# A new hand-written order of work in a fused attention and token-mixing kernel: first load ahead of the identity, q of the last batch loaded ahead of its k

## The chip, the cores and the metric

The kernel runs on one core of one Trainium2 chip. The metric is the time of one execution on the device in microseconds (us), as the median of three runs. Before the change it is 103.11 us (102.85 to 103.24).

The core has five engines with a queue each. TensorE (PE) multiplies matrices and writes to PSUM, an accumulator memory of eight banks. VectorE (DVE) and ScalarE (ACT) do the elementwise work and empty PSUM. GpSimd (POOL) does elementwise work in SBUF, the main on-chip memory. SyncE (SP) here only issues transfers. Each engine works through its queue in order and waits there until what the next instruction needs is done. Transfers (DMA) run beside the engines.

## What is computed

```
# per batch b (4) and head h (8); S = 768 rows, D = 64, 8 blocks of 96 rows
P = sort_net; five times: P = exp(P - rowmax); P /= rowsum; P /= columnsum   # 8x8, Sinkhorn
k_sorted = P @ k over blocks;   v_sorted = P @ v over blocks
attn = softmax(q_block @ k_sorted_block^T / 8)                               # inside a block
x[b, :, h] = attn @ v_sorted_block                                           # x: 768 x 512
# token mixing per batch
wq = x @ w_q;  wk = x @ w_k                                                  # 768 x 64
mixed = (wq @ wk^T / 8) @ x
out = relu(mixed) @ w_out                                                    # 768 x 512, float32
```

The inputs q, k and v are float32, 1.5 MB per batch each; the loads turn them into bf16.

## The kernel before

All work is cut into small **units**, and a table of words, `ORDER` (lines 17 to 46), says in which order they are recorded. A word such as `K30:0` has a kind (`K`), the batch (3), a number (0), and behind the colon what it works with. Capital kinds are matmuls on PE, and their number behind the colon is the PSUM bank. Small kinds empty the bank: `k30:A:0` empties bank 0 on ACT (`D` is DVE, `G` is POOL). `R`, `D` and `s` with `:S` are transfers that SP issues, and words with `l` are loads that POOL issues: `lq3` is q of batch 3, `lp` the two small mixing weights, `lo` the output weight. The order on each engine is the order of the table, restricted to that engine. Nothing reorders it later.

For one batch the units run as follows.

- `c`, `a` (batch-independent, at the start): the Sinkhorn iterations on a 32 x 64 tile `Pm`, on DVE (`c`, lines 167 to 181) and ACT (`a`, line 157), one waiting for the other. The last `c` leaves `PbT`. `B` and `n` spread it into the matrices `M` (lines 217 to 240), which every sorting matmul needs.
- `Q`/`q`: PE turns q of a pair of heads round, the result goes to `QT`. `K`/`k`: PE sorts k with `M`, into `KT`. `V`/`v`: the same for v, into `Vs`. Six `R` transfers (line 299) then bring `Vs` into blocks, `VT`. Batch 0 takes another way for v, by PE alone (`Y`, `y`, `F`, `f`).
- For batch 3, q is not turned by PE. POOL regroups it in four copies (`C`, line 358, into the buffer of another batch's q), and SP turns each copy round by a DMA transpose (`D34` to `D37`, line 362) into `QT`.
- `S`/`e`: scores and their exponential, seven units (E tile). `P`/`r`/`x`: attention times v, the reciprocal of the row sum, the normalised x; five units. `T`/`t`: x turned round, by PE, for batch 3 by DMA transposes (`D30` to `D33`).
- `J`/`j`/`d`, `W`/`w`, `G`/`g`, `H`/`h`, `O`/`o`: the token mixing, the last of them the output matmul, six units of four 128x512 matmuls. `s` stores to DRAM.

`Z` units are filler matmuls on a zero tile `fil`, whose results nobody reads. There are 28 of them, all in the first 14 us. `i00` makes the identity `idb` on POOL, `i02` clears tiles on DVE (`fil` among them), `i03` clears tiles on POOL.

There are three buffers for q, k and v each, so the loads of batch 3 go to the buffers of batch 0. All loads are issued by POOL, in the table's order: q0 v0 k0, v1, k1, q1, weights, q2 v2, output weight, k2, v3, k3, q3.

Of the kernel before, what the change touches and what calls it, by code (L numbers as in the profile page):

```python
# [16 lines left out]
ORDER = """
i00:G lq0 lv0 c00:D p01:A i02:D a01:A lk0 Z03:0 c01:D Z03:0 i03:G B01:0 a02:A Z014:1 c02:D lv1 a03:A c03:D
a04:A c04:D Q02:1 Q00:2 Q03:7 a05:A Z08:3 p00:A:0 q00:A:2 c05:D q02:A:1 q03:A:7 B00:0 Q01:3 n00:D:0 n02:D:0
n01:D:0 Y02:6 n03:D:0 Y00:1 y02:A:6 u00:D:0 Y01:4 y00:D:1 n10:G Y03:6 y01:D:4 F02:0 y03:A:6 F00:1 lk1 q01:A:3  # L20
f02:D:0 n11:G f00:D:1 K00:6 K01:2 k00:A:6 K03:0 k01:D:2 K02:4 lq1 k03:A:0 S00:6 k02:D:4 S02:2 e00:A:6 lp S01:0
F03:4 e01:A:0 S04:6 f03:D:4 lq2 F01:5 e02:A:2 P00:0 f01:D:5 n21:G e04:A:6 S03:2 r00:D:0 S06:4 x00:D:0 e03:A:2
P01:6 lv2 e06:A:4 r01:D:6 S05:0 x01:D:6 n20:G P02:2 e05:A:0 V10:4 r02:D:2 v10:A:4 x02:D:2 P03:0 lo K13:6 lk2
r03:D:0 P04:4 k13:A:6 x03:D:0 K12:2 lv3 V11:6 k12:A:2 r04:D:4 T01:0 x04:D:4 T00:1 v11:A:6 K11:2 t00:D:1 K10:4
k11:A:2 t01:D:0 V12:6 lk3 T03:1 k10:A:4 T02:0 lq3 t03:A:1 Q13:2 t02:D:0 Q12:3 Q11:4 v12:A:6 n31:G q12:D:3
J01:0 q13:D:2 J00:3 R15:S q11:D:4 j01:A:0 n30:G R11:S S13:6 j00:D:3 S14:0 R14:S e13:A:6 Q10:4 d00:G W00:3
R10:S W01:5 e14:A:0 w00:D:3 S15:6 R13:S w01:D:5 G00:3 d01:D q10:D:4 e15:A:6 R12:S S12:0 S10:4 G01:3 e12:A:0
Q22:7 g00:D:3 e10:A:4 q22:D:7 H01:0 H00:2 Q20:6 h01:A:0 h00:D:2 S11:4 e11:A:4 H02:0 S16:2 h02:D:0 Q23:7
e16:A:2 V22:4 q23:A:7 V20:2 v22:D:4 V21:0 O00:7 v20:A:2 q20:D:6 O02:4 o00:D:7 R20:S O03:2 o02:A:4 v21:A:0
P14:6 P11:3 r14:D:6 O01:5 x14:D:6 o03:A:2 R22:S r11:D:3 P13:6 R25:S x11:D:3 o01:A:5 P12:0 R23:S Q21:2 r13:D:6  # L30
R21:S r12:D:0 K23:3 x13:D:6 q21:A:2 O04:5 R24:S k23:A:3 x12:D:0 K21:6 K20:2 k21:A:6 o04:D:5 P10:0 k20:A:2
S22:6 r10:D:0 T13:5 x10:D:0 e22:A:6 T11:4 K22:2 t11:D:4 t13:A:5 S26:0 S21:6 k22:D:2 T12:4 e26:A:0 T10:5
e21:A:6 V31:0 t12:D:4 t10:D:5 S20:2 S23:6 e20:A:2 J11:5 J10:4 e23:A:6 j11:D:5 v31:D:0 S24:2 j10:A:4 W11:5
P21:6 e24:A:2 W10:4 r21:D:6 R33:S S25:0 w11:D:5 w10:A:4 x21:D:6 P20:2 e25:A:0 R32:S O05:4 r20:D:2 x20:D:2
V32:0 o05:A:4 P22:6 v32:A:0 P24:4 d10:D C30:G r22:D:6 T20:2 r24:D:4 G10:3 x24:D:4 t20:A:2 C31:G D34:S K30:0
x22:D:6 P23:4 k30:A:0 d11:G G11:3 r23:D:4 D35:S x23:D:4 K31:6 g10:A:3 K32:0 k31:A:6 C32:G H10:2 R35:S k32:D:0
V30:4 h10:A:2 R34:S T23:7 C33:G v30:D:4 T21:6 D36:S t23:A:7 T22:0 O10:2 t21:A:6 t22:D:0 R31:S H11:3 o10:D:2
S31:0 R30:S S32:6 e31:A:0 h11:D:3 J20:5 D37:S J21:2 e32:A:6 H12:0 s00:S j21:D:2 S33:3 j20:A:5 s02:S K33:6
e33:A:3 d21:D s01:S d20:G W20:5 k33:D:6 O11:2 h12:A:0 w20:D:5 W21:3 o11:D:2 S36:4 S34:6 e36:A:4 P31:0 s10:S
e34:A:6 G20:2 r31:D:0 w21:D:3 x31:D:0 S35:4 P32:6 e35:A:4 G21:2 r32:D:6 x32:D:6 S30:0 g20:A:2 P33:3 e30:A:0  # L40
O15:2 r33:D:3 D31:S x33:D:3 P34:0 o15:A:2 O12:7 r34:D:0 D32:S x34:D:0 P30:2 o12:A:7 H21:4 r30:D:2 H20:0 D33:S
x30:D:2 O13:7 h20:A:0 O14:6 h21:A:4 o13:D:7 D30:S O20:0 o14:D:6 O23:7 s12:S o20:A:0 s11:S O22:6 o23:D:7 J30:0
o22:D:6 J31:7 j30:A:0 s21:S O21:6 j31:A:7 d31:G W30:7 W31:0 o21:A:6 w30:D:7 H22:3 w31:D:0 G30:7 d30:D s20:S
h22:A:3 G31:7 O25:0 g30:D:7 H32:6 o25:D:0 H30:2 H31:4 h32:A:6 h30:D:2 O24:1 O34:7 o24:A:1 h31:D:4 O35:0 s22:S
o34:D:7 O30:4 o35:A:0 s34:S O33:7 s35:S o30:A:4 O32:0 s30:S o33:D:7 O31:4 s33:S o32:D:0 s32:S o31:D:4 s31:S
"""


# [605 lines left out]
```

## Time and profile before

| | us |
|---|---|
| median of three runs | 103.11 (102.85 to 103.24) |
| the profiled execution | 103.77 |
| its span in the profile | 101.9 |
| PE busy | 88.3 |
| DVE busy | 71.0 |
| ACT busy | 66.5 |
| POOL busy | 31.1 |

The profile follows one execution. The span runs from the first to the last record; 1.9 us of the execution lie outside it. An engine's busy time is the time in which at least one of its instructions ran; a matmul's end is modelled, so it can hold short waits. Times in the rows count from the start of the span. The lines that matter follow in the prediction.

### The profile page before, as it was taken

The page shows a single profiled execution, that of the slowest core. Times are in us where ns is not written, and L with a number is a line of the kernel's source. Part 1 is how long each engine was busy: PE and PEld are TensorE (multiplying, and loading weights), DVE is VectorE, ACT ScalarE, POOL GpSimd, SP SyncE. Part 2 cuts the span into 40 slices and gives each one's busy share as a digit, 9 for nine tenths or more (in the row PEclk, how much of TensorE's full clock was granted, in tenths as well). Part 3 has the DMA queues.
Part 4 walks back from the last instruction along what each step waited for, and adds up shares of the span by engine and source line. Part 5 has one row for each costly group of instructions (what it writes and reads, how often), then busy time and mean ns, then how long its engine had stood idle before and what let it go on. Part 6 is the DMA issues. An engine that isn't in the chain of part 4 may idle for free.

```text
span 101.9 us, 3335 instructions
## 1 busy us (share of the span) xinstructions
PE 88.3 (87%) x1403; PEld 60.0 (59%) x1412; DVE 71.0 (70%) x143; ACT 66.5 (65%) x92; POOL 31.1 (31%) x50
## 2 busy tenths in 40 slices
PE   0799989988998998799999999995799999999900
PEld 0234657887896676647687789753576544644300
DVE  0776559969976358928995899984769854477520
ACT  7212537999997699836799988975687653644200
POOL 7940007999969500000000006801000000860000
PEclk9999999999999999999999999999999999999998
DMA  0799999999999999999999991656998979824980
GB/s 3 71 193 203 203 206 206 184 192 204 198 194 202 203 225 245 247 204 222 218 242 240 205 220 31 130 134 143 264 413 302 119 160 361 357 113 175 346 308 6
DMA packets 25281, 20.63 MB, mean 202 GB/s; under 512 B 8240, under 2 KB 23344, under 8 KB 25264
## 3 DMA queue, kind: packets, MB, share of 16 engines
q0 software_dynamic: 14064, 10.09, 66.0%
q1 hardware_dynamic: 11200, 10.31, 33.4%
q8 instruction: 11, 0.18, 0.7%
q14 instruction: 6, 0.05, 0.1%
HBM read 20.19 MB, written 6.29 MB: 260 GB/s over the span
## 4 chain that ended last, share of the span: by engine, by line
DMA 46%; PE 33%; POOL 5%; DVE 4%; issue 3%; ACT 2%; SPq 1%; POOLq 0%; DVEq 0%
DMA Qn<-in_q_dram 41%; PE ps L142 33%; DMA QT<-Qn 4%; POOL M L238 3%; ACT mixT L417 2%; POOL Kn L214 2%; DMA Pm<-in_sort_net_dram 2%; DVE M L238 1%; DVE ot L148 1%; SPq L300 1%; POOL Qn L359 1%; POOL qD L380 1%; DVE PTR L148 0%; DVE KT L148 0%; DVE fil L190 0%
## 5 line engine op out<-in xcount | busy, mean ns | idle before, releaser
L314 ACT ACTIVATE E<-ps 96x960 bf16<-96x960 f32 (+1 forms) x28 | 23.6, 904 | 3.5 <-PE ps L142 3.5
L142 PE MATMUL ps<-wo,mixT 128*128 128x512 bf16 x88 | 22.0, 379 | 1.1 <-DMA wo<-in_moe_w_out_dram 0.6
L343 DVE TENSOR_TENSOR X<-ps,Rall 96x896 bf16<-96x896 f32 (+1 forms) x20 | 19.9, 1003 | 0.5
L142 PEld LDWEIGHTS <-mixT 128*128 128x128 bf16 x96 | 8.6, 97 | 10.4 <-DMA wo<-in_moe_w_out_dram 0.8
L148 DVE COPY ot<-ps 128x512 f32<-128x512 f32 x13 | 9.0, 690 | 5.3 <-PE ps L142 5.0
L146 ACT CAST KT<-ps 128x768 bf16<-128x768 f32 x13 | 10.2, 801 | 3.2 <-PE ps L142 2.9
L142 PE MATMUL ps<-fil 128*128 128x512 bf16 x27 | 9.1, 502 | 3.3 <-DVE fil L190 3.2
L142 PEld LDWEIGHTS <-KT 64*128 64x128 bf16 (+1 forms) x288 | 8.9, 97 | 5.0 <-issue 3.3
L359 POOL COPY Qn<-Qn 128x768 bf16<-128x768 bf16 x4 | 3.2, 826 | 26.8 <-DMA Qn<-in_q_dram 26.8
L142 PE MATMUL ps<-VT,E 96*128 96x65 bf16 x256 | 10.8, 193 | 0.4 <-ACT E L314 0.3
L142 PE MATMUL ps<-QT,KT 64*128 64x96 bf16 x256 | 9.4, 204 | 1.9 <-DMA QT<-Qn 1.1
L238 POOL TENSOR_TENSOR M<-PTR,m_p 128x512 bf16<-128x512 bf16 x6 | 7.9, 1330 | 9.7 <-DVE PTR L148 9.6
L142 PEld LDWEIGHTS <-E 96*128 96x128 bf16 x256 | 9.5, 97 | 2.3 <-issue 0.5
L146 ACT COPY ot<-ps 128x512 f32<-128x512 f32 x11 | 6.5, 588 | 6.5 <-PE ps L142 6.5
L380 POOL COPY qD<-qkT 64x384 bf16<-64x384 bf16 x4 | 2.0, 500 | 21.3 <-ACT qkT L146 20.4
L417 ACT ACTIVATE mixT<-ps 128x1024 bf16<-128x1024 f32 x7 | 7.0, 1021 | 2.2 <-PE ps L142 2.1
L142 PEld LDWEIGHTS <-fil 128*128 128x128 bf16 x28 | 3.1, 120 | 7.6 <-DVE fil L190 3.2
L148 DVE CAST KT<-ps 128x768 bf16<-128x768 f32 x7 | 6.5, 951 | 1.5 <-PE ps L142 1.5
L142 PE MATMUL ps<-M,Kn 128*64 128x128 bf16 x192 | 7.4, 221 | 0.0
L338 DVE RECIPROCAL Rall<-ps 96x14 f32<-96x14 f32 (+1 forms) x20 | 4.4, 226 | 3.2 <-PE ps L142 3.0
L142 PEld LDWEIGHTS <-Kn 128*64 128x64 bf16 x192 | 6.0, 109 | 1.0 <-issue 0.4
L146 ACT CAST Vs<-ps 128x1024 bf16<-128x1024 f32 x6 | 6.1, 1021 | 0.5 <-DMA VT<-Vs 0.4
(79 smaller groups left out, 136.2 us busy)
## 6 DMA issues: line engine op xcount, KB each, us to landing
out_dram<-ot SPq DMA_DIRECT2D x9, 512.0 KB, 3.3
Qn<-in_q_dram POOLq DMA_DIRECT2D x4, 768.0 KB, 11.2
Vn<-in_v_dram POOLq DMA_DIRECT2D x4, 768.0 KB, 15.3
Kn<-in_k_dram POOLq DMA_DIRECT2D x4, 768.0 KB, 16.9
VT<-Vs SPq DMA_DIRECT2D x18, 132.0 KB, 6.6
out_dram<-ot SPq DMA_DIRECT2D x6, 256.0 KB, 2.4
wo<-in_moe_w_out_dram POOLq DMA_DIRECT2D x1, 512.0 KB, 16.9
wqk<-in_moe_w_q_dram POOLq DMA_DIRECT2D x1, 64.0 KB, 9.5
```

The lines of the kernel that those rows point to most:

```text
L142: nc.tensor.matmul(o, w, x, is_transpose=t, start=start, stop=stop, skip_group_check=True)
L146: nc.scalar.copy(o, i)
L148: nc.vector.tensor_copy(o, i)
L214: nc.gpsimd.dma_start(out=t[b % NIN][:, h0:h1].rearrange("p h r d -> p h (r d)"), in_=src[b, h0:h1].rearrange("h (p r) d -> p h (r d)", p=P))
L238: ENG[e].tensor_tensor(out=M[b % 2][:, h0:h0 + hn], in0=src.unsqueeze(2).to_broadcast([P, hn, SP, NB]), in1=m_p.unsqueeze(1).unsqueeze(3). ...
L300: ENG[e].dma_start(out=VT[b % 2].rearrange("(s r) i h x -> r s i (h x)", r=R6)[n], in_=Vs[0][:, n].rearrange("p h e -> p (h e)"))
L314: nc.scalar.activation(E[b % 2][:, n, 0:2 * w * BLK].rearrange("p (t a c) -> p a t c", a=2, c=BLK), PS[0:BLK, bank:bank + 2, 0:w * BLK].re ...
L338: nc.vector.reciprocal(Rall[:, b, n, :, 0:w], avps(bank, w)[:, :, :, D])
L343: nc.vector.tensor_mul(xo.rearrange("p (a t d) -> p a t d", a=2, d=D), avps(bank, w)[:, :, :, 0:D], Rall[:, b, n, :, 0:w].unsqueeze(3).to_ ...
L359: nc.gpsimd.tensor_copy(pairs(b, n).rearrange("p (r h d) -> p r h d", r=R6, h=2), Qn[b % NIN][:, 2 * n:2 * n + 2].rearrange("p h r d -> p ...
L380: nc.gpsimd.tensor_copy(o, i)
L417: nc.scalar.activation(o, i, ACT.Relu)
```

## The change

The table is written anew: the order of the units, their banks and the engines that empty them. No function is touched, and the work is the same but for the fillers, of which there are 22 instead of 28. Of the evictions, ACT takes 17 of the 24 output evictions `o` (11 before) and DVE 7; ACT takes all four `y` (two before), five of eight `w` (one), two of eight `d` (none) and seven of nine `v` (six); DVE takes eight of sixteen `k` (five before), nine of twelve `t` (seven) and five of eight `j` (three). The word-for-word change of the table's first and last lines:

```diff
-i00:G lq0 lv0 c00:D p01:A i02:D a01:A lk0 Z03:0 c01:D Z03:0 i03:G B01:0 a02:A Z014:1 c02:D lv1 a03:A c03:D
+i02:D lq0 Z03:0 c00:D i00:G Z03:0 a01:A lv0 c01:D p01:A lk0 Z03:0 a02:A lv1 c02:D Z04:0 lk1 a03:A c03:D i03:G
...
-o34:D:7 O30:4 o35:A:0 s34:S O33:7 s35:S o30:A:4 O32:0 s30:S o33:D:7 O31:4 s33:S o32:D:0 s32:S o31:D:4 s31:S
+s22:S O34:7 o35:D:0 O30:4 s35:S o34:A:7 O33:0 s34:S o30:D:4 O32:7 s30:S o33:A:0 O31:4 s33:S o32:A:7 s32:S
+o31:A:4 s31:S
```

Three places show what moves. The first is POOL's queue at the start of the program. Before:

```order
L185 MEMSET idb_115 128x128
L186 ISA
L186 AFFINE_SELECT idb_115<-idb_115 128x128
L214 DMA Qn0_69<-in_q_dram 128x8x384
L214 DMA Vn0_75<-in_v_dram 128x8x384
L214 DMA Kn0_72<-in_k_dram 128x8x384
L195 MEMSET E0_87 96x7x32
```

And with the change (line numbers are one higher throughout):

```order
L215 DMA Qn0_69<-in_q_dram 128x8x384
L186 MEMSET idb_115 128x128
L187 ISA
L187 AFFINE_SELECT idb_115<-idb_115 128x128
L215 DMA Vn0_75<-in_v_dram 128x8x384
L215 DMA Kn0_72<-in_k_dram 128x8x384
L215 DMA Vn1_76<-in_v_dram 128x8x384
L215 DMA Kn1_73<-in_k_dram 128x8x384
L196 MEMSET E0_87 96x7x32
```

The load of q for batch 0 now stands ahead of the two instructions that make the identity, and the loads of v and k for batch 1 ahead of the clearing of tiles.

The second place is POOL's queue from the load of q for batch 2 (before) or from the load of k for batch 2 (after) up to the last load; buffers 0 to 2 of `Qn`, `Kn`, `Vn` hold batches 0 to 2, and batch 3 goes to buffer 0 again. Before:

```order
L214 DMA Qn2_71<-in_q_dram 128x8x384
L238 TENSOR_TENSOR M0_107<-PTR_110,m_p_116 128x512
L214 DMA Vn2_77<-in_v_dram 128x8x384
L238 TENSOR_TENSOR M0_107<-PTR_110,m_p_116 128x512
L209 DMA wo_79<-in_moe_w_out_dram 128x4x512
L214 DMA Kn2_74<-in_k_dram 128x8x384
L214 DMA Vn0_75<-in_v_dram 128x8x384
L214 DMA Kn0_72<-in_k_dram 128x8x384
L214 DMA Qn0_69<-in_q_dram 128x8x384
```

With the change:

```order
L239 TENSOR_TENSOR M0_107<-PTR_110,m_p_116 128x512 x2
L215 DMA Kn2_74<-in_k_dram 128x8x384
L210 DMA wo_79<-in_moe_w_out_dram 128x4x512
L215 DMA Vn2_77<-in_v_dram 128x8x384
L215 DMA Qn2_71<-in_q_dram 128x8x384
L215 DMA Vn0_75<-in_v_dram 128x8x384
L215 DMA Qn0_69<-in_q_dram 128x8x384
L215 DMA Kn0_72<-in_k_dram 128x8x384
```

Batch 2 is loaded as k, v, q instead of q, v, k, the output weight one place further forward; of batch 3, q now comes second and k last.

The third place is SP's queue from the last two `R` transfers that stand ahead of the first transpose of q for batch 3. Before:

```order
L300 DMA VT1_86<-Vs0_84 16x8x528 x2
L364 DMA_TRANSPOSE QT1_81<-Qn1_70 128x6x128 x2
L300 DMA VT1_86<-Vs0_84 16x8x528 x2
L364 DMA_TRANSPOSE QT1_81<-Qn1_70 128x6x128
L300 DMA VT1_86<-Vs0_84 16x8x528 x2
L364 DMA_TRANSPOSE QT1_81<-Qn1_70 128x6x128
L435 DMA out_0_dram<-ot0_103 128x1024
```

With the change:

```order
L301 DMA VT1_86<-Vs0_84 16x8x528 x2
L365 DMA_TRANSPOSE QT1_81<-Qn1_70 128x6x128
L301 DMA VT1_86<-Vs0_84 16x8x528
L365 DMA_TRANSPOSE QT1_81<-Qn1_70 128x6x128
L301 DMA VT1_86<-Vs0_84 16x8x528
L365 DMA_TRANSPOSE QT1_81<-Qn1_70 128x6x128
L301 DMA VT1_86<-Vs0_84 16x8x528 x2
L365 DMA_TRANSPOSE QT1_81<-Qn1_70 128x6x128
L436 DMA out_0_dram<-ot0_103 128x1024
```

The four transposes keep their place between the same transfers, roughly; what they wait for, the load of q for batch 3, is no longer the last load. On PE, the last load is waited for by `K30`. Behind `K30` the table now has 58 of PE's units, 61 before: `P23`, `T21`, `T22` and `V30` moved ahead of it, `T20` behind it.

More of the change, by code (lines that the diff above doesn't have):

```diff
@@ L17 @@
 ORDER = """
-i00:G lq0 lv0 c00:D p01:A i02:D a01:A lk0 Z03:0 c01:D Z03:0 i03:G B01:0 a02:A Z014:1 c02:D lv1 a03:A c03:D
[L19 to L42, printed above, removed]
@@ L43 @@
-o22:D:6 J31:7 j30:A:0 s21:S O21:6 j31:A:7 d31:G W30:7 W31:0 o21:A:6 w30:D:7 H22:3 w31:D:0 G30:7 d30:D s20:S
-h22:A:3 G31:7 O25:0 g30:D:7 H32:6 o25:D:0 H30:2 H31:4 h32:A:6 h30:D:2 O24:1 O34:7 o24:A:1 h31:D:4 O35:0 s22:S
-o34:D:7 O30:4 o35:A:0 s34:S O33:7 s35:S o30:A:4 O32:0 s30:S o33:D:7 O31:4 s33:S o32:D:0 s32:S o31:D:4 s31:S
+i02:D lq0 Z03:0 c00:D i00:G Z03:0 a01:A lv0 c01:D p01:A lk0 Z03:0 a02:A lv1 c02:D Z04:0 lk1 a03:A c03:D i03:G
+Z03:0 lq1 a04:A c04:D Q03:0 Q02:7 Q01:6 q03:D:0 a05:A Z06:5 c05:D Q00:5 B01:0 q00:D:5 B00:1 p00:A:0 q02:A:7
@@ new lines @@
+n01:D:1 n02:D:1 q01:A:6 Y01:4 n00:D:1 n03:D:1 y01:A:4 Y00:2 u00:D:1 Y03:6 Y02:4 n10:G y03:A:6 F01:0 y02:A:4
+F03:7 f01:D:0 lp y00:A:2 f03:D:7 K01:0 K00:2 k01:A:0 n11:G K03:6 k00:D:2 K02:4 k03:A:6 S02:0 k02:D:4 F02:2
+n21:G e02:A:0 S01:6 f02:D:2 S06:3 e01:A:6 S00:0 n20:G F00:5 e06:A:3 V12:6 f00:D:5 e00:A:0 S04:2 lk2 v12:D:6
+P01:4 e04:A:2 S05:0 lo r01:D:4 e05:A:0 R15:S P00:6 x01:D:4 lv2 S03:2 R14:S V10:0 e03:A:2 r00:D:6 lq2 P03:4
+x00:D:6 v10:A:0 P04:2 lv3 r03:D:4 r04:D:2 K12:6 x03:D:4 P02:0 k12:A:6 x04:D:2 V11:4 r02:D:0 T03:7 x02:D:0
@@ new lines @@
+v11:A:4 T00:6 K11:2 t00:D:6 T01:0 R12:S lq3 k11:A:2 t03:D:7 T02:4 R11:S t01:A:0 Q13:6 Q11:7 lk3 R10:S Q12:5
+t02:A:4 q11:D:7 Q10:0 R13:S K13:1 q10:A:0 J00:7 n31:G q12:A:5 S12:3 j00:D:7 J01:0 e12:A:3 k13:D:1 d00:G W00:7
+j01:A:0 q13:D:6 K10:3 w00:A:7 d01:D n30:G k10:A:3 S14:0 S13:6 W01:2 e13:A:6 w01:D:2 K21:3 G00:2 e14:A:0
+k21:D:3 S10:6 e10:A:6 K22:0 K20:3 k22:D:0 G01:2 k20:A:3 S11:6 g00:D:2 K23:0 e11:A:6 H01:2 k23:D:0 h01:A:2
+P12:4 S16:6 S15:0 r12:D:4 e16:A:6 x12:D:4 P10:2 e15:A:0 O03:7 r10:D:2 x10:D:2 o03:A:7 V22:0 H00:4 v22:A:0
@@ new lines @@
+V20:6 h00:D:4 P11:2 v20:A:6 R25:S V21:0 r11:D:2 H02:4 x11:D:2 v21:A:0 R20:S P13:6 R21:S h02:A:4 r13:D:6 P14:0
+x13:D:6 T11:2 R23:S Q20:3 R24:S Q21:4 r14:D:0 q20:A:3 Q23:7 R22:S q21:D:4 Q22:6 x14:D:0 S21:3 q22:A:6 O05:5
+q23:D:7 e21:A:3 t11:D:2 T13:7 S22:0 t13:D:7 S20:3 e22:A:0 T12:6 O04:7 t12:D:6 e20:A:3 T10:6 o04:A:7 S24:0
+t10:D:6 S26:2 O00:4 e26:A:2 o05:D:5 e24:A:0 V30:6 o00:A:4 S23:2 v30:D:6 S25:0 J10:5 e25:A:0 J11:4 R31:S
+j10:A:5 P21:0 e23:A:2 R30:S d10:G W10:7 V32:5 r21:D:0 j11:A:4 x21:D:0 P23:2 w10:A:7 O02:4 v32:A:5 C31:G
@@ new lines @@
+r23:D:2 x23:D:2 P22:0 d11:A C33:G o02:A:4 P20:6 W11:5 r22:D:0 V31:2 x22:D:0 C30:G w11:A:5 D37:S O01:4 v31:A:2
+C32:G r20:D:6 P24:0 x20:D:6 T22:5 o01:A:4 T21:2 R35:S t22:A:5 G10:3 r24:D:0 t21:D:2 D36:S K30:6 x24:D:0 K32:4
+k30:A:6 G11:3 k32:D:4 K33:0 R33:S g10:A:3 K31:6 k33:A:0 D35:S H10:2 k31:D:6 T20:4 h10:A:2 T23:5 S35:0 R34:S
+t23:D:5 S34:6 e35:A:0 H12:2 t20:D:4 R32:S O10:5 D34:S h12:A:2 J20:0 o10:D:5 e34:A:6 J21:1 j20:D:0 s00:S S36:4
+s02:S S32:2 j21:D:1 S33:6 e36:A:4 s01:S W20:0 e32:A:2 d21:G P33:4 w20:D:0 d20:G O11:0 e33:A:6 r33:D:4 x33:D:4
@@ new lines @@
+W21:1 P34:2 w21:A:1 P32:6 r34:D:2 o11:A:0 x34:D:2 S31:4 G20:1 s10:S e31:A:4 r32:D:6 D33:S x32:D:6 S30:2 G21:1
+H11:4 g20:A:1 D32:S P31:6 e30:A:2 O14:0 r31:D:6 x31:D:6 h11:A:4 P30:1 O15:3 o14:A:0 r30:D:1 D31:S x30:D:1
+O12:0 o15:A:3 D30:S H20:6 o12:D:0 H22:2 H21:4 h20:A:6 O13:1 h21:D:4 O20:0 h22:D:2 O23:7 o20:A:0 o13:A:1 J31:2
+o23:D:7 s11:S J30:0 s12:S j31:D:2 O22:7 j30:D:0 d31:D d30:A W31:0 W30:2 o22:A:7 O21:1 w30:D:2 w31:A:0 s21:S
+G30:0 o21:D:1 G31:0 s20:S O25:7 g30:A:0 H32:0 o25:A:7 H30:2 H31:4 h32:D:0 h30:A:2 O24:6 O35:0 o24:A:6 h31:A:4
```

## The prediction

> **What bounds the kernel now.** I read the page first, for the share of each engine, then the chain that ended last, then stretches of the span and PE's waits in them.
>
> ```profile
> PE 88.3 (87%) x1403; PEld 60.0 (59%) x1412; DVE 71.0 (70%) x143; ACT 66.5 (65%) x92; POOL 31.1 (31%) x50
> ```
>
> PE is busy for 87% of the span, so it must be followed stage by stage. The chain of waits, in order of time (start, length, what):
>
> ```profile
> 30.53 31.43 DMA Qn<-in_q_dram
> ...
> 66.99 3.74 DMA QT<-Qn
> ...
> 96.96 0.69 DVE ot L148
> ```
>
> The last load, q of batch 3, is issued at 30.53 and lands at 61.96. Then POOL regroups it, SP transposes it, and the last transpose lands at 70.73. The chain is released by PE's last output matmul at 96.96.
>
> The next view cuts the span at 61.75, where PE starts `K30`, the first unit on batch 3's k (first row, from PE's timeline), and at 96.93, PE's end. Columns: stretch, length, busy time of PE, PEld, DVE, ACT, POOL, granted clock, DMA share, GB/s. Below it PE's waits in 61.6 to 97.4 (total, times, longest).
>
> ```profile
> 61.75 0.50 PE L142 MATMUL ps<-M,Kn 128*64 128x128 bf16 x12
> ```
>
> ```profile
> 19.42:61.75 42.33, 39.94 (x808) 31.14 (x809) 32.98 (x58) 36.25 (x48) 14.15 (x16) 1.00 1.28 214
> 61.75:96.93 35.18, 32.97 (x401) 19.82 (x401) 24.61 (x39) 21.54 (x30) 7.96 (x14) 1.00 0.72 220
> ```
>
> ```profile
> PE ps L142 <- DMA QT<-Qn: 1.1, 1, 1.1
> PE ps L142 <- DVE ot L148: 0.5, 1, 0.5
> ```
>
> Two regimes. Up to the last load the DMA engines are full (share 1.28) and PE, at 39.94 of 42.33, hardly waits: the work keeps pace with the loads. Behind it PE works off what is left, busy for 32.97 of 35.18, and its one long wait is for the transposed q. The end is the later of PE's arrival at batch 3 and the last load, plus PE's remaining work. The sum has these three terms, each for the changed kernel.
>
> **Term 1: when the last load lands.** POOL's rows at the start:
>
> ```profile
> 0.74 0.20 POOL L185 MEMSET idb<- 128x128 bf16 x1 [0.29 <-POOLq L638]
> 1.02 0.29 POOL L186 TENSOR_SCALAR_AFFINE_SELECT idb<-idb 128x128 bf16<-128x128 bf16 x1
> 1.46 1.13 POOL L214 DMA_DIRECT2D Qn<-in_q_dram  x1
> ```
>
> With the first load ahead of the identity it is issued at 0.74, not 1.46: the stream starts 0.72 us earlier. The identity comes about 1.2 us later, under the load's own travel and the Sinkhorn steps. The stream never runs dry in either order (the share above), so its end moves as its start, as long as no more is moved beside it. But more is. The rows are issues by POOL (k and q of batch 1, k and q of batch 3), SP's `R` issues, and of the same four loads the us from issue to landing:
>
> ```profile
> 17.17 0.94 POOL L214 DMA_DIRECT2D Kn<-in_k_dram  x1
> ...
> 19.39 0.94 POOL L214 DMA_DIRECT2D Qn<-in_q_dram  x1
> ...
> 29.67 0.88 POOL L214 DMA_DIRECT2D Kn<-in_k_dram  x1 [0.93 <-DMA Qn<-in_q_dram]
> 30.53 0.89 POOL L214 DMA_DIRECT2D Qn<-in_q_dram  x1
> ```
>
> ```profile
> 32.70 26.32 SPq L300 DMA_DIRECT2D VT<-Vs  x14
> ```
>
> ```profile
> Kn<-in_k_dram POOLq DMA_DIRECT2D x1, 768.0 KB, 8.4
> ```
>
> ```profile
> Qn<-in_q_dram POOLq DMA_DIRECT2D x1, 768.0 KB, 10.0
> ```
>
> ```profile
> Kn<-in_k_dram POOLq DMA_DIRECT2D x1, 768.0 KB, 27.9
> ```
>
> ```profile
> Qn<-in_q_dram POOLq DMA_DIRECT2D x1, 768.0 KB, 31.4
> ```
>
> Alone, a load follows the one ahead of it after 3.8 us (25.57 to 29.39). The last one took 4.4 (57.57 to 61.96), with the last two of the 14 `R` beside it: some 0.3 us for each `R`. In the new order of SP's queue, about 16 `R` and two of the four q transposes fall before the last load lands, since q now lands one load earlier, near 57, and POOL's first copy and SP follow at once. What a transpose costs shows where two ran nearly alone:
>
> ```profile
> 62.50:66.40 3.90, 3.76 (x79) 3.15 (x77) 3.77 (x5) 3.45 (x6) 3.29 (x5) 1.00 0.48 92
> ```
>
> ```profile
> 62.96 2.65 SPq L364 DMA_TRANSPOSE QT<-Qn  x2
> ```
>
> 0.48 of 3.90 us is 1.87, or 0.94 a transpose, and at the loads' share of 1.28 that displaces 0.73 us of load. So the last load, now k, lands at 61.96 - 0.72 + 2 x 0.3 + 2 x 0.73 = 63.3. The bounds are 61.2 (transfers beside the load cost it nothing) and, should transposes hold it up for their whole time of 3.90 / 2, far later (the rival on the slow side).
>
> **Term 2: when PE reaches `K30`.** The start first, on DVE, then on PE:
>
> ```profile
> 11.68 0.23 DVE L181 STREAM_TRANSPOSE PbT<-Pb 32x64 bf16<-32x64 bf16 x1
> 14.01 1.42 DVE L238 TENSOR_TENSOR M<-ps,m_p 128x256 bf16<-128x256 f32 x4 [2.10 <-PE ps L142]
> ```
>
> ```profile
> 3.17 2.74 PE L142 MATMUL ps<-fil 128*128 128x512 bf16 x6 [3.17 <-DVE fil L190]
> ...
> 11.93 1.67 PE L142 MATMUL ps<-fil 128*128 128x512 bf16 x7 [0.16 <-issue]
> ```
>
> ```profile
> L148 DVE COPY QT<-ps 128x768 bf16<-128x768 bf16 x6 | 3.2, 553 | 0.3 <-PE ps L142 0.3
> ```
>
> `PbT` is ready at 11.91, but eight fillers stand ahead of `B00` on PE, so DVE gets to `M` only at 14.01. In the new table the last six fillers stand ahead of `Q00`, where `PbT` isn't ready yet. On the other hand DVE gets two q evictions of 0.553: one stands in the Sinkhorn chain, of which I count 0.3 (the rest is under an ACT step), the other right ahead of `M`. So `M` starts near 11.91 + 0.3 + 0.55 = 12.8, 1.2 us earlier. The next stage is a chain of evictions on ACT, which now has all four `y`; I keep 1.0 us of the gain (bounds 0 and 1.4). The clearing of tiles ahead of the first Sinkhorn step, on DVE, is hidden by the wait for the sort matrix; uncovered, it would shift `M` by its own length, which the lower bound takes in.
>
> Then the middle. Ahead of `K30` there are now also `P23`, `T21`, `T22` and `V30`, and `T20` no longer:
>
> ```profile
> L142 PE MATMUL ps<-VT,E 96*128 96x65 bf16 x256 | 10.8, 193 | 0.4 <-ACT E L314 0.3
> ...
> L142 PE MATMUL ps<-Vn,M 128*128 128x128 bf16 x72 | 5.2, 219 | 0.1
> L142 PE MATMUL ps<-idb,X 96*128 96x96 bf16 x96 | 5.1, 206 | 0.0
> ```
>
> 14 x 0.042 + (2 - 1) x 8 x 0.053 + 8 x 0.072 = 0.59 + 0.42 + 0.58 = 1.6 us more ahead of it.
>
> ```profile
> 43.09 1.25 PE L142 MATMUL ps<-wo,mixT 128*128 128x512 bf16 x4 [0.63 <-DMA wo<-in_moe_w_out_dram]
> ```
>
> The wait of 0.6 for the output weight goes, since one load less (some 4 us) stands ahead of it. PE reaches `K30` at 61.75 - 1.0 + 1.6 - 0.6 = 61.75, as before, and then waits for k until 63.3, for 1.5 us. That wait is new and takes the place of the 1.1 us for the transposed q.
>
> In this stretch ACT gets one more each of `h`, `j`, `o`, `v` and `d` and two more `w`, while of the equally large `q` and `k` it has one less in all.
>
> ```profile
> L146 ACT CAST Vs<-ps 128x1024 bf16<-128x1024 f32 x6 | 6.1, 1021 | 0.5 <-DMA VT<-Vs 0.4
> ```
>
> `v` and `h` empty 1024 columns, 1.02 each; the other five are smaller; so between 1 and 5 us more, I take 3.3. ACT is idle for 42.33 - 36.25 = 6.1 us there, so I count nothing; half of that idle time gone is a rival.
>
> **Term 3: what is left behind `K30`.** The units behind it are the same but for those 1.6 us. Without any idle time PE needs 32.97 - 1.6 = 31.4; with all of it but the waits for q and the output eviction, 35.18 - 1.6 - 1.1 - 0.5 = 32.0. I take 31.7. The transposed q isn't late any more: its first two pieces land near 63, the last near 68, and the scores that need the last one stand some 9 us behind `K30`.
>
> **The sum.** PE ends at 63.3 + 31.7 = 95.0 instead of 96.93, and the last eviction is now on ACT, 0.1 shorter: 2.0 us less. The profiled execution, 103.77, would be 101.8; the median shown is 0.66 lower, so **101.1**.
>
> **Rivals.**
>
> - *The loads aren't held up.* R and transposes find room beside k. Then the load lands at 61.2, PE's arrival at 61.75 decides, the end is 93.5: 3.6 less, **99.5**. For it: a share of 0.48 while two transposes run. Against it: the 4.4 us of the last load.
> - *ACT becomes the bound of the middle.* If its 3.3 us don't fit in, PE reaches `K30` at 65.0 and ends at 96.7: **102.8**, no change that can be seen. For it: 36.25 of 42.33 is already much.
> - *Slower: transposes hold up the loads.* If each stops k for 1.95 us and so draws the next one in front of the landing, four cost 7.8, k lands at 69.6, the end is 101.3, **107.4**. It decides from a landing at 65.8 on, 1.0 us for each of four transposes. Against it: half of the share is free while they run. The Trainium skill (DMA: Bandwidth & Descriptors, Queues, rings and completion order) says that a DMA engine takes turns between its queues packet by packet; by that a transpose costs the load only its own packets, and this rival falls. No run here shows the two side by side yet.
> - *A cold PE.* The first fillers took 2.74 / 6 = 0.46 us each, later ones 1.67 / 7 = 0.24: PE starts at half speed. If its new wait makes it fall back for as long as those six, 1.3 us are lost: **102.4**. Against it:
>
> ```profile
> 70.00:75.00 5.00, 3.67 (x67) 2.73 (x67) 2.36 (x7) 3.06 (x4) 0.50 (x1) 1.00 0.87 263
> ```
>
> PE idled 1.33 us here and the clock stayed at 1.00. The Trainium skill (TensorE: Matmul & The Clock Gate, Part 1) puts the idle time that throttles the clock at about 3.4 us; by that a wait of 1.5 is harmless.
>
> **How the numbers follow.** Forecast 0.58, loads not held up 0.17, ACT 0.14, transposes 0.07, cold PE 0.04. The range, 99.0 to 103.0, holds the forecast with a us or so for the bounds of term 1 and the start, and most of the first two rivals. 0.5%, 0.5 us, is about what a measurement tells from no change. Faster by more than that: forecast, first rival and cold PE, less the forecast's upper edge, 0.75; within it: ACT and that edge, 0.17; slower: 0.08.
>
> **What would show it.** First load issued near 0.74; `M` on DVE near 12.8; the last load landing near 63.3, issued by POOL for k; one wait of PE for `Kn` of 1 to 2 us at about 62 and none for `QT`; PE's end near 95. The forecast is wrong if k lands before 62 or after 65, if PE reaches `K30` after k has landed, or if PE's idle time behind `K30` is over 1 us.

## The result, and the profile after

| | before | after |
|---|---|---|
| median, runs of the same chip (us) | 103.17 (102.85 to 103.33, 4 runs) | 99.84 (99.79 to 100.31, 4 runs) |
| ratio to before | | 0.9689, interval 0.9657 to 0.9722 |
| profiled execution | 103.77 | 100.31 |
| its span | 101.9 | 98.5 |

The change makes the kernel 3.1% faster. The forecast was 101.1 us, with 99.0 to 103.0 as its range.

The page of the changed kernel, busy time of each engine:

```profile
PE 87.1 (88%) x1406; PEld 58.9 (60%) x1406; DVE 66.4 (67%) x133; ACT 70.8 (72%) x102; POOL 31.0 (31%) x50
```

PE is busy for 1.2 us less (there are six fillers fewer), DVE for 4.6 less and ACT for 4.3 more: the evictions that changed hands. Next the stretches of its span, cut as before at the first score matmul (17.99 now, 19.42 before), at the first matmul of `K30` (62.36 now, its row below, 61.75 before) and at PE's end (93.99 now, 96.93 before). Columns as in the prediction.

```profile
17.99:62.36 44.37, 41.29 (x839) 32.25 (x838) 33.91 (x56) 40.03 (x54) 15.94 (x18) 1.00 1.30 214
62.36:93.99 31.63, 31.17 (x376) 17.92 (x372) 20.64 (x32) 21.56 (x33) 4.18 (x9) 1.00 0.85 240
```

```profile
62.36 0.84 PE L143 MATMUL ps<-M,Kn 128*64 128x128 bf16 x24
```

Up to `K30` PE did 1.35 us more (41.29 against 39.94), started 1.43 earlier and still arrived 0.61 later. The gain is behind `K30`: 31.63 instead of 35.18, and busy for 31.17 of them. From 61.75 + 35.18 to 62.36 + 31.63 is 2.94 of the 3.4 us of span; the other 0.46 lies behind PE's last matmul, in the last eviction (0.59 on ACT, 0.69 on DVE before) and the store.

PE's waits in the changed kernel, two rows of the list:

```profile
PE ps L143 <- DMA Vn<-in_v_dram: 1.1, 2, 0.7
...
PE ps L143 <- DMA VT<-Vs: 0.4, 1, 0.4
```

The waits for `QT`, for `wo` and for the output eviction are gone; there are two for v, of batch 1 and of batch 2, and none for the k of batch 3. The chain that ended last:

```profile
22.78 19.90 DMA Vn<-in_v_dram
...
46.28 16.61 PE ps L143 x312
...
69.87 24.12 PE ps L143 x232
...
94.01 0.59 ACT ot L147
```

Before, it went back through the transposes to the *last* load. Now it goes back to the load of v for batch 2, which lands at 22.78 + 19.90 = 42.68. That is the place where PE last runs dry for a load, the first unit on that v, `V22`:

```profile
42.72 0.62 PE L143 MATMUL ps<-Vn,M 128*128 128x128 bf16 x8 [0.47 <-DMA Vn<-in_v_dram]
```

At nearly the same moment, 43.09, the kernel before waited for `wo`. Both kernels meet the stream of loads within 0.4 us of each other, whatever came ahead. The other wait for v is for batch 1, whose first unit starts at 24.95 in the kernel before:

```profile
21.09 0.61 PE L143 MATMUL ps<-Vn,M 128*128 128x128 bf16 x8 [0.65 <-DMA Vn<-in_v_dram]
```

From the meeting near 43 on, PE is busy almost without a gap up to `K30` in both kernels, though the DMA engines stay full there. The stretch before, then with the change:

```profile
43.09:61.75 18.66, 18.48 (x341) 13.62 (x345) 14.82 (x28) 14.78 (x22) 0.00 (x0) 1.00 1.23 218
```

```profile
42.72:62.36 19.64, 19.33 (x360) 14.76 (x362) 15.06 (x26) 17.86 (x26) 3.62 (x5) 1.00 1.27 214
```

Three steps of the prediction hang on POOL, DVE and SP. First POOL's first load, then the last one with its us from issue to landing, and DVE's first `M`:

```profile
1.27 1.13 POOL L215 DMA_DIRECT2D Qn<-in_q_dram  x1 [0.82 <-POOLq L639]
...
30.86 0.88 POOL L215 DMA_DIRECT2D Kn<-in_k_dram  x1
```

```profile
Kn<-in_k_dram POOLq DMA_DIRECT2D x1, 768.0 KB, 31.3
```

```profile
12.57 1.42 DVE L239 TENSOR_TENSOR M<-ps,m_p 128x256 bf16<-128x256 f32 x4
```

The first load is issued at 1.27, not 0.74. The last lands at 30.86 + 31.3 = 62.16, just before PE gets to it. And SP's queue from 56 to 70, with POOL's four copies of q of batch 3:

```profile
58.62 1.32 SPq L365 DMA_TRANSPOSE QT<-Qn  x1
60.05 1.75 SPq L301 DMA_DIRECT2D VT<-Vs  x1
61.89 1.29 SPq L365 DMA_TRANSPOSE QT<-Qn  x1
```

```profile
57.00 3.13 POOL L360 COPY Qn<-Qn 128x768 bf16<-128x768 bf16 x4 [0.24 <-DMA Qn<-in_q_dram]
```

The transpose that stands first in SP's queue needs the second copy, so it is issued at 58.62, 1.6 us behind the first copy's start, and the second one, behind an `R` that takes 1.75 us of SP, only at 61.89. One transpose falls beside the load of k, not two.

### The profile page after: what moved, and what is told of

It is laid out like the page before. It is cut to its first block, busy times and chain, and to the rows that moved or that the text cites. A ratio compares the mean times of both kernels' runs of the same rounds, so it can differ in the third digit from the quotient of the medians.

```text
span 98.5 us, 3326 instructions
## 1 busy us (share of the span) xinstructions
PE 87.1 (88%) x1406; PEld 58.9 (60%) x1406; DVE 66.4 (67%) x133; ACT 70.8 (72%) x102; POOL 31.0 (31%) x50
## 4 chain that ended last, share of the span: by engine, by line
PE 47%; DMA 32%; POOL 8%; ACT 5%; SPq 2%; issue 2%; ACTq 0%; POOLq 0%
PE ps L143 47%; DMA Vn<-in_v_dram 20%; DMA Qn<-in_q_dram 8%; POOL M L239 5%; DMA VT<-Vs 4%; ACT KT L147 2%; POOL wqk L208 2%; SPq L365 1%; ACT QT L147 1%; ACT Vs L147 1%; POOL Kn L215 1%; POOL wo L210 1%; SPq L301 1%; ACT ot L147 1%; ACT m_p L147 0%
## 5 line engine op out<-in xcount | busy, mean ns | idle before, releaser
L143 PE MATMUL ps<-wo,mixT 128*128 128x512 bf16 x96 | 23.4, 380 | 0.0
L147 ACT COPY ot<-ps 128x512 f32<-128x512 f32 x17 | 9.9, 586 | 4.8 <-PE ps L143 4.3
L147 ACT CAST KT<-ps 128x768 bf16<-128x768 f32 x12 | 9.4, 801 | 1.4 <-PE ps L143 1.0
L149 DVE CAST KT<-ps 128x768 bf16<-128x768 f32 x8 | 7.6, 955 | 2.2 <-PE ps L143 2.2
L143 PE MATMUL ps<-fil 128*128 128x512 bf16 x22 | 7.8, 530 | 1.2 <-DVE fil L191 1.2
L418 ACT ACTIVATE mixT<-ps 128x1024 bf16<-128x1024 f32 x8 | 8.2, 1025 | 0.6 <-PE ps L143 0.6
L147 ACT CAST Vs<-ps 128x1024 bf16<-128x1024 f32 x7 | 6.9, 1017 | 1.1 <-PE ps L143 1.0
L149 DVE COPY ot<-ps 128x512 f32<-128x512 f32 x7 | 4.8, 690 | 4.1 <-PE ps L143 3.8
L143 PE MATMUL ps<-Vn,M 128*128 128x128 bf16 x72 | 5.5, 219 | 1.3 <-DMA Vn<-in_v_dram 1.1
L420 DVE TENSOR_SCALAR mixT<-ps 128x1024 bf16<-128x1024 f32 x4 | 4.8, 1222 | 2.6 <-PE ps L143 2.4
```

The costliest lines, as they stand in the source:

```text
L143: nc.tensor.matmul(o, w, x, is_transpose=t, start=start, stop=stop, skip_group_check=True)
L147: nc.scalar.copy(o, i)
L149: nc.vector.tensor_copy(o, i)
L418: nc.scalar.activation(o, i, ACT.Relu)
L420: nc.vector.tensor_relu(o, i)
```

## The experiments

**1. The exchange of q and k undone, all else as changed.**

```diff
-... R12:S lq3 k11:A:2 ... Q11:7 lk3 R10:S Q12:5
+... R12:S lk3 k11:A:2 ... Q11:7 lq3 R10:S Q12:5
```

> The changed kernel with the last two loads exchanged again: k of batch 3 ahead of its q. Theory 1 (q ahead of k removes a wait of the tail): q lands last at about 62, the second of POOL's copies ends near 63.7, the first transpose lands near 67 instead of 63, so PE waits for QT by 1.4 us or more at the first score unit of batch 3 and again for later pieces; 1.5 to 3 us slower than the changed kernel: 101.3 to 102.8. Rival (the exchange is hidden, the gain is the rest of the new order): PE finds other work, within 0.5 us of the changed kernel: 99.5 to 100.3.

105.16 us (104.5 to 106.04), ratio 1.0174 (1.0111 to 1.0237): slower than the kernel before. PE reaches `K30` at 62.32 as with the change, and then waits twice for the transposed q. PE's rows, then two stretches of the span:

```profile
66.00 0.39 PE L143 MATMUL ps<-QT,KT 64*128 64x96 bf16 x10 [0.62 <-DMA QT<-Qn]
69.03 0.42 PE L143 MATMUL ps<-QT,KT 64*128 64x96 bf16 x6 [2.65 <-DMA QT<-Qn]
```

```profile
64.84:68.25 3.41, 0.93 (x23) 0.72 (x20) 1.52 (x3) 1.82 (x2) 0.00 (x0) 1.00 0.92 128
68.25:75.07 6.82, 6.04 (x46) 2.90 (x48) 1.81 (x3) 2.21 (x3) 0.00 (x0) 0.50 0.82 230
```

The waits themselves are 3.3 us. The rest is the granted clock: it drops to 0.50 inside the second wait and stays there for 6.82 us, in which PE was busy for 6.04, work of some 3.0 us at full clock. So 3.3 + 3.0 = 6.3 us would be lost; 5.7 us of span are. By the medians the loss is 5.3 us, where 1.5 to 3 were expected: that estimate had the waits and not the clock. The new table can't do without the exchange; that this is because it moved units of PE (`P23`, `T21`, `T22`, `V30`) away from just that place is argued, not shown. The mechanism of the prediction's cold PE is real, with a longer wait than the one forecast.

**2. The exchange alone, in the kernel before.**

```diff
-... lk3 T03:1 k10:A:4 T02:0 lq3 ...
+... lq3 T03:1 k10:A:4 T02:0 lk3 ...
```

> The kernel before with only the last two loads exchanged: q of batch 3 ahead of its k. Theory 1: the wait for QT (1.1 us) and what follows from it go, but PE now reaches K30 at 61.6 and k lands at 62 to 63: 0.5 to 1.6 us faster than before, 101.6 to 102.7. Rival (transposes beside the last load hold it up by 0.7 us or more each): no gain or slower, 103 or more.

101.84 us (101.57 to 102.64), ratio 0.9883 (0.9832 to 0.9934). Its stretches, cut at its own first scores, `K30` and PE's end, and its longest wait behind the start:

```profile
18.29:61.47 43.18, 39.97 (x810) 30.98 (x809) 33.06 (x57) 36.30 (x48) 17.82 (x21) 1.00 1.31 218
61.47:95.09 33.62, 32.98 (x406) 19.78 (x401) 24.90 (x39) 21.46 (x30) 4.27 (x9) 1.00 0.78 226
```

```profile
PE ps L142 <- DMA wo<-in_moe_w_out_dram: 1.8, 1, 1.8
```

The wait for `QT` is gone and 33.62 us are left behind `K30` instead of 35.18, with the same work. By the medians that is 1.2 of the 3.1%. Beside it the changed kernel shows where the other part comes from: it reaches `K30` 0.9 later (62.36), but with about 1.6 us of units moved ahead of it, and has 31.63 left, 2.0 less. PE's end is 1.1 earlier. Its start was hardly earlier (17.99 and 18.29): what it has instead is less idle time up to `K30`, 44.37 - 41.29 = 3.1 against 43.18 - 39.97 = 3.2, for a stretch that holds 1.3 us more work, and 0.46 of it idle behind, against 0.64.

Two more things stand in this trace. `M` comes at 12.87, where the kernel before, with the same words up to there, has it at 14.01; so the start differs by over 1 us from one execution to the next:

```profile
12.87 1.42 DVE L238 TENSOR_TENSOR M<-ps,m_p 128x256 bf16<-128x256 f32 x4 [0.88 <-PE ps L142]
```

And the first two transposes of q are issued before the last load has landed, at 58.92 and 60.35. That load, issued at 29.94, still lands at 60.94, 1.0 earlier than the last load of the kernel before:

```profile
58.92 3.98 SPq L364 DMA_TRANSPOSE QT<-Qn  x2
```

```profile
Kn<-in_k_dram POOLq DMA_DIRECT2D x1, 768.0 KB, 31.0
```

**3. The identity ahead of the first load again.**

```diff
-i02:D lq0 Z03:0 c00:D i00:G Z03:0 ...
+i02:D i00:G lq0 Z03:0 c00:D Z03:0 ...
```

> The changed kernel with the identity ahead of the first load again (and behind the clearing of tiles on DVE). In the changed trace the first load was issued at 1.27, not at 0.74, and landed at 8.67 (before: 1.46 and 9.26). Theory 1 (the loads set the pace to v of batch 2, for which PE waits, so a later stream shifts all): q lands 0.4 to 0.6 us later and so does the end: 100.2 to 100.5. Rival (PE's own pace decides): no change, 99.8.

99.97 us (99.58 to 100.86), ratio 0.9686 (0.9643 to 0.9730): no difference from the change. The load goes out at 1.46 instead of 1.27; `V22` starts at 42.88 instead of 42.72, `K30` at 62.49 instead of 62.36.

**4. Why the first load doesn't go out at 0.74: DVE's clearing put behind its first steps.**

```diff
-i02:D lq0 Z03:0 c00:D i00:G Z03:0 a01:A lv0
+lq0 c00:D i02:D Z03:0 i00:G Z03:0 a01:A lv0
```

> The changed kernel with DVE's clearing of tiles (i02) behind DVE's first Sinkhorn step instead of ahead of everything, the load of q still first on POOL. In the changed kernel the first load is issued at 1.27, while DVE clears tiles from 0.80 to 1.32. Theory: that issue needs about half a us on POOL for itself, whatever DVE does: it stays at 1.2 to 1.3, time as the changed kernel within 0.5. Rival: it waits for DVE's clearing to end; then it comes at 0.75 to 0.85, q0 lands 0.4 earlier, and every load behind it too (v of batch 2 at 42.3).

99.82 us (99.69 to 100.0), ratio 0.9673 (0.9613 to 0.9734). POOL's first load, and DVE's clearing (four `MEMSET`s in three rows), which now runs far behind it:

```profile
1.27 1.13 POOL L215 DMA_DIRECT2D Qn<-in_q_dram  x1 [0.82 <-POOLq L639]
```

```profile
2.84 0.07 DVE L190 MEMSET Pm<- 32x8 f32 x1
2.90 0.27 DVE L191 MEMSET fil<- 128x256 uint32 x1
3.14 0.18 DVE L193 MEMSET KT<- 128x64 uint32 x2
```

1.27 to the hundredth: DVE is not what it waits for. Some half a us passes on POOL ahead of the first load whatever stands in front; behind the identity, most of it is hidden (1.46). The rival falls.

**5. The start alone: the kernel before without its eight fillers ahead of `B00`.**

```diff
-a04:A c04:D Q02:1 Q00:2 Q03:7 a05:A Z08:3 p00:A:0 ...
+a04:A c04:D Q02:1 Q00:2 Q03:7 a05:A p00:A:0 ...
```

> The kernel before without the eight filler matmuls that stand ahead of B00. M starts on DVE some 1.5 us earlier (12.5 instead of 14.0). Theory 1 (the loads set the pace later): PE catches up with the loads and waits for them; gain of 0 to 0.4 us: 102.8 to 103.2. Rival (PE's pace decides from the start on): the 1.5 us arrive at the end: 101.7.

103.16 us (102.54 to 104.59, 12 runs), ratio 0.9976 (0.9937 to 1.0015): no change that can be seen. `M` on DVE, and two of PE's waits:

```profile
12.50 1.42 DVE L238 TENSOR_TENSOR M<-ps,m_p 128x256 bf16<-128x256 f32 x4 [0.61 <-PE ps L142]
```

```profile
PE ps L142 <- DMA QT<-Qn: 1.6, 1, 1.6
PE ps L142 <- DMA wo<-in_moe_w_out_dram: 1.5, 1, 1.5
```

`M` comes 1.5 us earlier, as early as with the change, and the wait for `wo` grows from 0.6 to 1.5, that for `QT` from 1.1 to 1.6: together 1.4. The head start is given back, nearly all of it, at the two places where PE meets the loads. A part of the 1.5 belongs to the execution and not to the fillers, since `M` was at 12.87 with them in experiment 2; there too the wait for `wo` was longer, 1.8.

**6. The start alone, the other way: eight fillers ahead of `B00` in the changed kernel.**

```diff
-... Q00:5 B01:0 q00:D:5 B00:1 ...
+... Q00:5 B01:0 Z08:3 q00:D:5 B00:1 ...
```

> The changed kernel with eight more filler matmuls on PE right ahead of B00, the place where the kernel before has its eight (8 x 0.24 = 1.9 us at full clock, part of it under the wait for PbT). M on DVE would start near 14, some 1.4 us later than the 12.57 of the changed kernel. Theory: a head start of PE is worth nothing, since PE meets the load stream again at V22, whose v lands at 42.7 whatever PE does: V22 at 42.7 to 43.2, K30 at 62.2 to 62.8, time 99.6 to 100.5. Rival: the start counts in full, PE reaches V22 and K30 about 1.4 us later and the time is about 101.2.

100.53 us (100.1 to 102.05), ratio 0.9728 (0.9665 to 0.9791). Between the two: 0.7 us above the changed kernel by the medians, half of the start's 1.4, 0.4 by the ratios, and the intervals overlap. The execution that was profiled is the one of 102.05, with the clock at half speed in part of the start and `M` at 16.24, so its trace doesn't tell how late `M` was in the others. In this one `M` is 3.67 later than in the changed kernel, `V22` (44.72) 2.00 and `K30` (64.37) 2.01 later, with no wait for a load on the way: 1.67 us were taken in ahead of `V22` and nothing behind it. What a late start of 1.4 costs the changed kernel stays open between nothing and the 1.4.

**7. The order of the other two loads, in the kernel before: with the exchange, and `wo` ahead of v of batch 2.**

```diff
-... lk3 T03:1 k10:A:4 T02:0 lq3 ...
+... lq3 T03:1 k10:A:4 T02:0 lk3 ...
...
-... P01:6 lv2 e06:A:4 ... P03:0 lo K13:6 ...
+... P01:6 lo e06:A:4 ... P03:0 lv2 K13:6 ...
```

> The kernel before with q of batch 3 ahead of its k, and the output weight ahead of v of batch 2, as the changed kernel has both; units as before. Theory: PE meets the stream near 42.7 at whichever unit needs the load that lands then, so only the units that stand ahead of that wait count. The wait for wo (1.8 with the exchange of q and k alone) goes, but V22, which PE reaches at 39.5, waits for v until about 42.5, some 3 us, with less work ahead of it: 0.8 to 1.5 us slower than with the exchange alone, 102.6 to 103.3. Rival: the wait for wo was the loss, and the new order of these two loads alone wins it back: 100.2 to 101.2.

104.4 us (104.15 to 105.87), ratio 1.0166 (1.007 to 1.0261). PE's row for `V22`, and two stretches around it:

```profile
43.14 2.74 PE L142 MATMUL ps<-Vn,M 128*128 128x128 bf16 x24 [2.65 <-DMA Vn<-in_v_dram]
```

```profile
39.19:42.60 3.41, 1.14 (x22) 0.68 (x19) 1.75 (x2) 2.14 (x4) 0.00 (x0) 1.00 1.24 250
42.60:46.01 3.41, 2.87 (x25) 2.69 (x26) 1.69 (x2) 0.90 (x1) 0.00 (x0) 0.50 1.31 202
```

The wait for `wo` has become a longer one for v, at the same place in time, with less work done ahead of it: the rival, that this order wins by itself, falls. The price is larger than expected, 2.6 us against the exchange alone instead of 0.8 to 1.5, and the second row says why: the clock was at 0.50 for 3.41 us, in which PE's 2.87 were worth half. Without those 1.4 some 1.2 is left, as expected. So this order of the two loads doesn't pay without the new order of units.

**8. Does the last load set `K30`? Only heads 0 to 3 of k of batch 3 loaded.**

```diff
-... Q11:7 lk3 R10:S Q12:5
+... Q11:7 lk3a R10:S Q12:5
```

> The changed kernel with only heads 0 to 3 of the last load (k of batch 3), so that it lands some 2 us earlier, near 60; the other heads use what the buffer holds of batch 0, which leaves out half of that load. Theory A (the last load gates K30, and with it the end): K30 starts 1 to 2 us earlier and the time falls by as much, 98 to 99. Theory B (PE arrives at K30 at 62.3 from what holds it at 42.7, the wait for v of batch 2, and the last load only just doesn't matter): K30 at 62.0 to 62.4, time 99.5 to 99.9.

99.67 us (99.62 to 101.0), ratio 0.9693 (0.9626 to 0.9759). The half load, issued at 30.86, with its us to landing, and PE's first matmul on it:

```profile
Kn<-in_k_dram POOLq DMA_DIRECT2D x1, 384.0 KB, 27.9
```

```profile
62.27 0.84 PE L143 MATMUL ps<-M,Kn 128*64 128x128 bf16 x24
```

The load lands at 58.76, 3.4 earlier, and PE begins `K30` at 62.27 instead of 62.36. The last load doesn't hold PE up; PE's own arrival sets the end.

**9. What a DMA transpose costs beside the loads: four more of them on SP from 40.5 on** (a sorted k tile into a part of `QT` that batch 3 overwrites later).

```diff
-... P12:4 S16:6 S15:0 r12:D:4 ...
+... P12:4 S16:6 S15:0 tx r12:D:4 ...
...
+        if kind == "t" and item == "tx":
+            for m in range(4):
+                nc.sync.dma_start_transpose(out=QT[1][:, m], in_=KT[0][:, 3, 0:S])
```

> The changed kernel with four more DMA transposes of 128x768 bf16 (SBUF to SBUF, into a buffer that is written again later) issued on SP from about 40.5 on, while only loads run, ahead of the R transfers of batch 2. It measures what a transpose costs the loads: q of batch 2 lands at 46.45 and v of batch 3 at 51.65 in the changed kernel. At my price of 0.73 each, v of batch 3 lands 2.9 us later, 54.5. At 0 it stays at 51.7; at the slow rival's 1.95 it lands near 59. The time: 0 to 3 us above the changed kernel's 99.84, as the later landings reach PE.

112.43 us (111.94 to 112.59), ratio 1.088 (1.0826 to 1.0935). The last load, issued at 30.95, with its us to landing; SP's queue, each of the four by itself; PE's longest wait:

```profile
Kn<-in_k_dram POOLq DMA_DIRECT2D x1, 768.0 KB, 34.9
```

```profile
40.51 1.32 SPq L611 DMA_TRANSPOSE QT<-KT  x1
41.94 2.50 SPq L611 DMA_TRANSPOSE QT<-KT  x1
44.53 4.20 SPq L611 DMA_TRANSPOSE QT<-KT  x1
48.82 4.82 SPq L611 DMA_TRANSPOSE QT<-KT  x1
53.73 1.87 SPq L301 DMA_DIRECT2D VT<-Vs  x3
```

```profile
PE ps L143 <- DMA VT<-Vs: 11.1, 1, 11.1
```

The last load lands at 65.85, 3.7 later: 0.9 us for each transpose, where the prediction took 0.73 and its slow rival 1.95. v of batch 3, which was to tell, lands at 53.40 instead of 51.65, 1.75 later: the rival's 59 isn't met. The price itself isn't settled, since what else moved beside the loads changed too: six `R` fell behind v of batch 3, and by the last landing three `R` and one transpose of q were missing, so that the 0.9 is rather too low. The time is lost elsewhere: next to the loads the four keep SP for 13.13 us, the later ones longest, and the `R` transfers behind them, issued from 44.4 on in the changed kernel, go out at 53.7. PE then waits 11.1 for `VT`, and the clock is at 0.50 from 61.2 to 71.4. The Trainium skill (DMA: Bandwidth & Descriptors, Queues, rings and completion order) has a DMA engine take turns between its queues packet by packet. The trace agrees for the load as far as it goes: by these landings a transpose cost it less than its own 1.95; the damage is in the order of SP's own queue, of which that rule says nothing.

**10. The gate moved: v of batch 2 ahead of the output weight, and one output unit, `O03`, behind it.**

```diff
-P01:4 e04:A:2 S05:0 lo r01:D:4 ... x01:D:4 lv2 S03:2 ...
+P01:4 e04:A:2 S05:0 lv2 r01:D:4 ... x01:D:4 lo S03:2 ...
-... O03:7 r10:D:2 x10:D:2 o03:A:7 V22:0 ... R21:S h02:A:4 r13:D:6 P14:0
+... r10:D:2 x10:D:2 V22:0 ... R21:S O03:3 h02:A:4 r13:D:6 o03:A:3 P14:0
```

> The changed kernel with v of batch 2 loaded ahead of the output weight, and the first output unit O03 with its eviction moved from ahead of V22 to behind P13 (bank 3), so that it does not wait for the weight. Theory B: the wait of PE for v at 42.7 goes (0.8 us with what hangs on it); the next landing, q of batch 2 at 46.5 against its use at 47.0, allows 0.4 of it: 99.4 to 99.7. Theory A: nothing changes, 99.8.

100.23 us (99.95 to 100.87), ratio 0.9703 (0.9667 to 0.9740): no gain. v now lands at 40.09, 2.6 earlier. `V22` on PE, and the evictions of E ahead of it on ACT:

```profile
42.47 0.61 PE L143 MATMUL ps<-Vn,M 128*128 128x128 bf16 x8 [0.64 <-ACT E L315]
```

```profile
41.08 1.34 ACT L315 ACTIVATE E<-ps 96x384 bf16<-96x384 f32 x2
```

`V22` starts 0.25 us earlier only: its bank isn't emptied before 41.08 + 1.34 = 42.42. The wait for v has become a wait for ACT, and `O03`, 1.0 us of PE that stood ahead of it, now stands behind; `K30` comes at 63.06, 0.7 later. So in the changed kernel the wait for v at 42.7 is worth no more than a few tenths: the bank would have held `V22` up nearly as long.

**11. The first transposes as early as they can be: POOL's copies in the order in which SP needs them, and SP's queue with two transposes, four `R`, two transposes.**

```diff
-... C31:G ... C33:G ... C30:G ... C32:G
-D37:S R35:S D36:S R33:S D35:S R34:S R32:S D34:S
+... C33:G ... C32:G ... C31:G ... C30:G
+D37:S D36:S R35:S R33:S R34:S R32:S D35:S D34:S
```

> The changed kernel with POOL's copies of q of batch 3 in the order in which the transposes need them (pair 3 first) and SP's queue as transpose, transpose, four R, transpose, transpose. In the changed trace P33 waits for the last R at 69.4 (0.4 us, with the gap ahead of it 0.5). If PE's work behind K30 decides, that wait goes: 0.3 to 0.5 us faster, 99.3 to 99.6. If the two early transposes hold up the last load (0.7 each), K30 waits and nothing is won or up to 0.7 lost: 99.8 to 100.5.

100.25 us (100.12 to 100.37), ratio 0.9707 (0.9674 to 0.9741). SP's first two transposes, and PE's wait behind `K30`:

```profile
57.84 2.70 SPq L365 DMA_TRANSPOSE QT<-Qn  x2
```

```profile
PE ps L143 <- DMA QT<-Qn: 0.6, 1, 0.6
```

Now two transposes do fall beside the load of k, as in experiment 2, and it lands at 61.26, no later than with one (62.16). `K30` starts at 62.11. The last transposes, which are later in the queue, cost a wait of 0.6: nothing is won.

## Why the prediction was right, and where it wasn't

**Term 3, what is left behind `K30`,** carried the gain, and was right: 31.7 forecast, 31.63 measured. The wait for `QT` (1.1) and that for the output eviction (0.5) are gone, and the 1.6 us of units that moved ahead of `K30` are missing behind it. Experiments 1 and 2 show the first part from both sides.

**Term 1, the last load, was too late by 1.1 us:** 63.3 forecast, 62.16 measured. The start of the stream gave 0.2 at the issue (1.27 for 1.46) and 0.6 at the landing of the first q, where 0.72 was taken. The load ahead of the last lands 0.7 earlier (56.9 against 57.57), but so it does, at 57.07 and 57.08, in experiments 2 and 5, whose first load goes out at 1.46: the early first load isn't shown to be the reason. The step that failed is what moves beside the last load and what that costs, 2.06 for two more `R` and two transposes. "Two of the four q transposes fall before the last load lands": one did, since the transpose at the head of SP's queue waits for POOL's second copy. And the price can't be seen at this place: the last load lands at 61.96 and 61.04 with no transpose beside it (the kernel before, experiment 5), at 62.16 and 61.43 with one (the change, experiment 4, the same queue), at 60.94 and 61.26 with two (experiment 2, where the second has only just begun, and experiment 11). Single executions differ by up to 0.9, and no price shows above that. In the middle of the stream experiment 9 shows one, some 0.9 or more for a transpose.

**Term 2, PE's arrival, was 0.6 too early:** 61.75 forecast, 62.36 measured. `M` came at 12.57 (12.8 forecast), and the first scores 1.43 earlier. But of that gain "I keep 1.0" was wrong in kind: the kernel before gives nearly all of it back where it meets the loads (experiment 5). How the changed kernel fares there, experiment 6 leaves open. "The wait of 0.6 for the output weight goes" held for that weight only; two waits for v, which the prediction doesn't have, took its place: 0.65 at 21.09 for batch 1, since the first unit on it comes earlier now, and 0.47 at 42.72 for batch 2 (with ACT's eviction right behind it, by experiment 10). By the trace's numbers, 61.75 - 1.43 + 1.6 - 0.6 + 1.1 = 62.4.

**So the new wait of 1.5 us for k never came.** The prediction named this as a sign of error: `K30` starts behind k's landing, by 0.2 us, and experiment 8 shows that a load 3.4 us earlier moves it by 0.1 only. The forecast had the larger of two times as 63.3; it was 62.36, set by the other one. That is 0.9 of the 1.5 us by which the profiled execution (100.31) lies under the 101.8 of the sum; 0.1 comes from term 3, and some 0.35 from the end behind PE, of which only 0.1 was counted. Which of the two times decides is what the first rival, loads that aren't held up, had in mind: PE's arrival decides. Its 99.5 is nearer to 99.84 than the forecast is, so in this point the likeliest case was chosen wrongly. That the time still lies in the range is owed to term 3 and to the width of the range; the forecast's own path, a wait for the last load, didn't occur.

**The other rivals.** ACT took 40.03 - 36.25 = 3.8 us more up to `K30` (3.3 forecast), in 44.37 us; PE's two waits for it there are 0.3 each, so it isn't the bound, though it is close at `V22` (experiment 10). Transposes that stop a load for their whole length fall with experiment 9. The cold PE didn't occur in the changed kernel, whose clock is 1.00 in both stretches; experiments 1 and 7 show that it was one load's order away.

**Where the gain came from, then.** The DMA engines are full up to about 62 us in both kernels (share 1.28 and 1.30), but PE waits for loads only up to about 43. From there to `K30` it is busy for 18.48 of 18.66 us before and 19.33 of 19.64 with the change, and the last load itself holds up the kernel before through the transposes only. The exchange removes that wait (1.2%, experiment 2). The rest comes with the new table: against experiment 2, PE ends 1.1 earlier in the traces, and the end behind PE is 0.5 shorter. The new order of units gives PE about 1.3 us more to do before `K30` for nearly the same idle time. That this is the cause of the rest is argued from the two kernels' stretches; no run here moved those units alone, and the start may hold a part of it (experiment 6). The early first load, named in the change, is worth nothing that can be measured (experiment 3).

## What to carry to other kernels

Where a stream of loads and then one engine set the time, read the profile as two stretches and ask of each edit which of the two it shortens: work moved out of the second into idle time of the first can be won, a head start ahead of the next meeting with the stream may count for nothing. The border between the two is the last load that the engine really waits for (here near 43), not the last load of the stream (62). An order of loads and an order of work are one decision; the exchange alone gained little more than a third of this change (experiment 2), the new table without it lost time (experiment 1). Before charging a queue's transfers to a load, follow what the first one in that queue itself waits for.
